# Five entries of a placement table: when the next expert's weight operands are made

## The chip, the cores and the metric

The kernel runs on one core of a Trainium2 chip. The metric is the device time of one execution in microseconds (us): before the change 1099.89 us, the median of three runs (1097.52, 1099.89, 1102.34).

## The reference

Three layers run one after the other on 2304 rows of 512 values. The first two (an attention with exponential features, and a mixture of experts over slots) are not touched. The third is:

```python
logits = x @ w_gate
P = np.exp(logits - logits.max())
for _ in range(8):                       # balancing
    P /= P.sum(1, keepdims=True) + 1e-09
    P /= P.sum(0, keepdims=True) + 1e-09
    P *= N / E
for e in range(E):                       # E = 8 experts, w1[e] 512 x 1024, w2[e] 1024 x 512
    h = np.maximum(x @ w1[e], 0.0)
    out += P[:, e:e + 1] * (h @ w2[e])
```

## The kernel before

**Experts and blocks.** The third layer goes through 8 experts (0 to 7), and through 9 blocks (0 to 8) of 256 rows in each; the code calls a place in it `(blk, k)`, block and product. The hidden block (1024 x 256) is laid out as 2 x 2 quarters, and `h @ w2` is done by a scheme of Strassen's kind: 7 products of sums of quarters in place of 8 products. `PRODUCTS` names for each product k = 0 to 6 the hidden operand, the weight operand and the accumulator:

```python
PRODUCTS = [("a11", "b11", "x"), ("a12", "b21", "z"), ("s2", "t2", "x"), ("s1", "t1", "y"),
            ("s3", "t3", "x"), ("s4", "b22", "y"), ("a22", "t4", "x")]
```

**Operands in two parts.** Each operand is a high part and a low part: ScalarE (ACT) writes the rounded copy, and the low part is the difference. A product is 12 matmuls (high x high, high x low, low x high, over 4 chunks). Four hidden operands (`s1`, `s2`, `s4`, `s3`, in this order) get their low part `hl_s` on GpSimd (POOL); the others, and the sums themselves, are made by VectorE (DVE), which also takes each finished product into the output (`take`: `xo <- x, P, xo`).

**Weight operands.** Those of the next expert are made while this one runs. `w_begin` allocates, `w_sum(e, n)` makes one of four sums t1 to t4 on POOL, in place in the loaded weights (t2 has a tile of its own), and `w_part(e, k)` makes operand k: an ACT copy (`CAST w_b` or `w_t`, 128x1024) and a POOL subtraction on the same tile. The profile's `w_b` are the operands b11, b21 and b22 (k = 0, 1, 5), its `w_t` are t2, t1, t3 and t4 (k = 2, 3, 4, 6). There are 10 operand buffers, and operand k of expert e has number `(7 * e + k) % 10`. So operand k of the next expert, for k = 3 to 6, goes to the buffer of this expert's operand k - 3, and must wait for its last product, which is product k - 3 of block 8.

**What sets the order.** From the middle of the kernel on every engine runs its instructions in the order in which the code writes them (`InOrder`); waits between engines are put in by the framework. The loop at the end of `tile_kernel` writes, for each product: the product and its take; at product 2 the first layer of the next block; one step of the next block's hidden operands (`hidden`); then the sums and operands that the two tables `W_SUMS` and `W_PARTS` name for this place. A key with block 9 is block 0 of the next expert. In block 8 the next expert's first-layer weights are stacked (`make_stack` behind product 0: `ps`, `st`) and spread (`spread_stack` behind product 1: `pr`, and two ACT copies `st <- pr`). While expert 0 runs, DVE also does the balancing of `P` (`sinkhorn`), a few steps at a time. After block 0 of an expert `load_munits` asks for further weights on the SyncE queue; each transfer waits until its buffer is free.

Of the kernel before, what the change touches and what calls it, by code (L numbers as in the profile page):

```python
# [53 lines left out]
def tile_kernel(ctx: ExitStack, tc: tile.TileContext, a):  # L54
# [569 lines left out]
    def w_sum(e, n):  # L624


        w = wsrc[e]
        if n == 0:
            G.tensor_tensor(out=w["t1"], in0=w["t3"], in1=w["b11"], op=ALU.subtract)
        elif n == 1:  # L630
            G.tensor_tensor(out=w["t2"], in0=w["t1"], in1=w["b22"], op=ALU.subtract)
        elif n == 2:
            G.tensor_tensor(out=w["t3"], in0=w["t3"], in1=w["b22"], op=ALU.subtract)
        else:
            G.tensor_tensor(out=w["t4"], in0=w["t4"], in1=w["t2"], op=ALU.add)

    def w_part(e, k):

        name = PRODUCTS[k][1]
        s = wsrc[e][name]  # L640
        n = (7 * e + k) % NW
        w = (cl1 if n < 4 else cl2).tile([128, 2, KH, 256], F32R, tag=f"wo{n}", name=f"w{e}_{name}", bufs=1)
        A.copy(out=w[:, 0], in_=s)
        G.tensor_tensor(out=w[:, 1], in0=s, in1=w[:, 0].bitcast(F32), op=ALU.subtract)
        wop[e, k] = w
        if k == 6:
            wsrc.pop(e)
            for n in range(2):
                unit_t.pop(("moe2_w2", e, n))
# [286 lines left out]
        pass  # L936
    load_munits(4)

    W_SUMS = {(3, 1): 0, (3, 6): 1, (5, 6): 2, (7, 6): 3}
    W_PARTS = {(2, 6): 0, (4, 6): 2, (6, 6): 1, (8, 1): 3, (8, 6): 4, (9, 0): 5, (9, 1): 6}  # L940
    SINK = {0: 1, 1: 2, 6: 2}
    making = iter(())
    for i, (e, blk) in enumerate(blocks):
# [3 lines left out]
        for k in range(7):  # L947
# [10 lines left out]
            next(making, None)  # L958
            if more and (blk, k) in W_SUMS:
                w_sum(e + 1, W_SUMS[blk, k])  # L960
            if more and (blk, k) in W_PARTS:
                w_part(e + 1, W_PARTS[blk, k])
            if e and (blk + 9, k) in W_PARTS:
                w_part(e, W_PARTS[blk + 9, k])
            if e == 0:
# [72 lines left out]
```

## Time and profile before

| | |
|---|---|
| runs (us) | 1102.34, 1097.52, 1099.89 |
| profiled execution | 1099.17 us, span 1097.0 us |
| granted clock of TensorE, mean | 0.994 |
| PE (matmuls) busy | 1053.4 us, 96% |
| DVE, ACT, POOL busy | 67%, 52%, 63% |
| third layer, products | from 281.2 us to the end |
| one `w_sum` or the POOL half of one `w_part` | 2.4 us |
| one `hl_s` pair on POOL | 2.5 to 2.6 us |

The profile shows one execution. Times are us from the start of the span. "PE" is matmuls, "PEld" the loads of their stationary operand, which overlap them. In a timeline a row is the start, the busy time, the engine, the line (all are line 50, a helper that records every operation), the operation, what it writes and reads, and in brackets the idle time of that engine just before it with what ended it. A chain of waits goes back from the end, at each step to what released it. The first-layer matmuls `z<-ct,st` come once per block, between its products 2 and 3, and serve as a mark for its place in time.

### The profile page before, as it was taken

How to read it: one execution, taken by the hardware profiler on the slowest of the kernel's cores; microseconds unless marked ns; L12 is line 12 of the kernel's file. 1: busy time of each engine (PE TensorE's matmuls, PEld its weight loads, DVE VectorE, ACT ScalarE, POOL GpSimd, SP SyncE). 2: the span in 40 equal slices, each digit the busy share in tenths (PEclk: the TensorE clock that was granted, in tenths of full speed). 3: DMA queues.
4: the chain of work that ended last, by engine and by line, in shares of the span. 5: the costliest groups of instructions: out<-in, count | busy, mean ns of one | idle time of the engine just before them, and what ended most of it. 6: DMA issues, size and time to landing. Idle time of an engine off the chain costs nothing.

```text
span 1097.0 us, 23161 instructions
## 1 busy us (share of the span) xinstructions
PE 1053.4 (96%) x9206; PEld 982.4 (90%) x9206; DVE 737.7 (67%) x1526; ACT 569.1 (52%) x1009; POOL 686.8 (63%) x442
## 2 busy tenths in 40 slices
PE   7999999999888899999999999999999999999998
PEld 4788889853888889999999999999999999999998
DVE  6878677750678866766776677567666766676765
ACT  5665544313455556655455455545554564555542
POOL 4776551107555676767767686867677775777443
PEclk9999989999999999999999999999999999999999
DMA  7762215379400040012002200400220022000111
GB/s 261 261 257 85 59 30 208 139 303 370 154 1 1 2 143 12 2 50 105 1 1 78 78 2 1 149 6 2 77 78 1 1 82 73 1 1 21 45 53 59
DMA packets 22571, 89.26 MB, mean 81 GB/s; under 512 B 2752, under 2 KB 5568, under 8 KB 14272
## 3 DMA queue, kind: packets, MB, share of 16 engines
q1 hardware_dynamic: 22176, 87.26, 22.0%
q8 instruction: 73, 1.20, 0.5%
q0 software_dynamic: 288, 0.52, 0.2%
q14 instruction: 34, 0.28, 0.1%
HBM read 83.05 MB, written 4.72 MB: 80 GB/s over the span
## 4 chain that ended last, share of the span: by engine, by line
PE 68%; POOL 15%; issue 6%; DVE 6%; ACT 4%; DMA 1%; SPq 0%; POOLq 0%; ACTq 0%; DVEq 0%
PE x L50 25%; PE y L50 12%; PE z L50 11%; POOL hl_s L50 8%; PE num L271 6%; POOL w_t L50 4%; PE kvacc L179 3%; POOL w_b L50 2%; DVE s L50 2%; PE ut L246 1%; PE ps L50 1%; PE kvp L218 1%; DMA moe_w<-in_moe_w 1%; ACT hh_s L50 1%; DVE xo L50 1%
## 5 line engine op out<-in xcount | busy, mean ns | idle before, releaser
L50 POOL TENSOR_TENSOR hl_s<-s,hh_s 128x512 fp32r<-128x512 f32 x288 | 367.4, 1297 | 240.9 <-ACT hh_s L50 226.5
L50 PE MATMUL x<-w_t,hh_s 128*128 128x256 f32 x1152 | 205.0, 278 | 5.2 <-DVE xo L50 3.9
L50 ACT ACTIVATE hh_s<-s 128x512 fp32r<-128x512 f32 x288 | 175.3, 629 | 52.0 <-DVE s L50 49.3
L50 PEld LDWEIGHTS x<-w_t,hh_s 128*128 128x128 f32 x1152 | 173.9, 188 | 7.2 <-issue 3.2
L50 DVE SCALAR_TENSOR_TENSOR xo<-x,P,xo 128x256 f32<-128x256 f32 x252 | 121.0, 480 | 81.0 <-PE x L50 75.4
L50 ACT ACTIVATE hh_a<-z 128x512 fp32r<-128x512 f32 x216 | 122.2, 600 | 90.5 <-DVE s L50 88.6
L50 ACT ACTIVATE r<-z 128x512 f32<-128x512 f32 x144 | 86.2, 599 | 159.9 <-PE z L50 159.6
L50 DVE SCALAR_TENSOR_TENSOR s<-z,r 128x512 f32<-128x512 f32 x144 | 99.0, 688 | 90.6 <-ACT hh_a L50 86.2
L50 PE MATMUL x<-w_t,hl_s 128*128 128x256 f32 x576 | 159.7, 277 | 0.0
L50 DVE SCALAR_TENSOR_TENSOR hl_a<-z,hh_a 128x512 fp32r<-128x512 f32 x216 | 147.2, 681 | 0.0
L50 DVE SCALAR_TENSOR_TENSOR s<-z,s 128x512 f32<-128x512 f32 x144 | 98.4, 684 | 20.6 <-POOL hl_s L50 19.3
L50 PE MATMUL x<-w_t,hh_a 128*128 128x256 f32 x576 | 104.3, 279 | 5.2 <-POOL w_t L50 4.8
L50 PEld LDWEIGHTS x<-w_t,hl_s 128*128 128x128 f32 x576 | 108.2, 188 | 0.0
L50 PE MATMUL y<-w_b,hh_s 128*128 128x256 f32 x576 | 103.9, 279 | 0.0
L50 PE MATMUL z<-w_b,hh_a 128*128 128x256 f32 x576 | 103.6, 280 | 0.0
L50 PE MATMUL x<-w_b,hh_a 128*128 128x256 f32 x576 | 103.4, 280 | 0.0
L50 PE MATMUL y<-w_t,hh_s 128*128 128x256 f32 x576 | 102.9, 278 | 0.0
L50 PEld LDWEIGHTS x<-w_t,hh_a 128*128 128x128 f32 x576 | 87.6, 188 | 6.8 <-POOL w_t L50 6.2
L50 PEld LDWEIGHTS z<-w_b,hh_a 128*128 128x128 f32 x576 | 87.3, 189 | 2.5 <-issue 2.5
L50 PEld LDWEIGHTS y<-w_b,hh_s 128*128 128x128 f32 x576 | 87.5, 188 | 1.3 <-POOL w_b L50 1.3
L50 PEld LDWEIGHTS x<-w_b,hh_a 128*128 128x128 f32 x576 | 88.0, 190 | 0.0
L50 PEld LDWEIGHTS y<-w_t,hh_s 128*128 128x128 f32 x576 | 87.6, 189 | 0.0
(214 smaller groups left out, 2344.7 us busy)
## 6 DMA issues: line engine op xcount, KB each, us to landing
moe_w<-in_moe_w SPq DMA_DIRECT2D x64, 1024.0 KB, 6.9
vt<-in_vb SPq DMA_DIRECT2D x20, 256.0 KB, 3.6
kt<-in_kT SPq DMA_DIRECT2D x18, 256.0 KB, 3.5
qt<-in_qT SPq DMA_DIRECT2D x18, 256.0 KB, 2.7
out<-xo SPq DMA_DIRECT2D x18, 128.0 KB, 1.7
out<-xo SPq DMA_DIRECT2D x9, 256.0 KB, 2.0
rep<-in_rep POOLq DMA_DIRECT2D x2, 256.0 KB, 6.0
bd<-in_bd SPq DMA_DIRECT2D x1, 384.0 KB, 3.7
```

Of the source, the lines that this page charges most:

```text
L50: return lambda *args, **kwargs: self.tc.keep_in_program_order(make(*args, **kwargs))
L179: PE.matmul(acc[64 * j:64 * j + 64, p * 256:(p + 1) * 256], v[:, (2 * p + j) * D:(2 * p + j + 1) * D], phik[:, 2 * p + j].rearrange("p c f ...
L218: PE.matmul(ps[:, c * 192:(c + 1) * 192], kvt[:, p * 256 + c * 128:p * 256 + (c + 1) * 128], bd[:, p], start=True, stop=True)
L246: PE.transpose(ps[:, j * 128:(j + 1) * 128], uq_t[t][hh][:, j * 128:(j + 1) * 128], ident)
L271: PE.matmul(ps[r0:r1, j * XW:(j + 1) * XW], phiq[:, c, j * 128 + r0:j * 128 + r1], kvs_t[b][:, c, 4 * hh + j, :], start=c == 0, stop=c == 1,)
```

## The change

The entries of the two tables are changed, and nothing else:

```diff
-    W_SUMS = {(3, 1): 0, (3, 6): 1, (5, 6): 2, (7, 6): 3}
-    W_PARTS = {(2, 6): 0, (4, 6): 2, (6, 6): 1, (8, 1): 3, (8, 6): 4, (9, 0): 5, (9, 1): 6}
+    W_SUMS = {(3, 1): 0, (3, 6): 1, (5, 6): 2, (7, 1): 3}
+    W_PARTS = {(2, 6): 0, (4, 6): 2, (6, 6): 1, (8, 0): 3, (8, 1): 4, (8, 6): 5, (9, 0): 6}
```

The last sum (t4) goes from product 6 of block 7 to product 1. Operand 3 (t1) goes from product 1 of block 8 to product 0, operand 4 (t3) from product 6 to product 1, operand 5 (b22) from product 0 of the next expert's block 0 to product 6 of block 8, operand 6 (t4) from product 1 of that block 0 to product 0.

On POOL, from the last low part that is made for block 8 of expert 3 to the first that is made for block 1 of expert 4 (`w4_...` are the weight operands of expert 4; `hl_s1_36` is the low part of s1 for the 36th block counted from 0, which is block 0 of expert 4). Before:

```order
L50 TENSOR_TENSOR hl_s3_35_8679<-s3_35_8661,hh_s3_35_8677 128x512
L50 TENSOR_TENSOR moe2_w2_4_1_7655<-moe2_w2_4_1_7655,t4_7805 128x4x256
L50 TENSOR_TENSOR w4_t1_8743<-moe2_w2_4_0_7653,w4_t1_8743 128x1024
L50 TENSOR_TENSOR hl_s1_36_8797<-s1_36_8774,hh_s1_36_8795 128x512
L50 TENSOR_TENSOR hl_s2_36_8816<-s2_36_8790,hh_s2_36_8814 128x512
L50 TENSOR_TENSOR hl_s4_36_8840<-s4_36_8820,hh_s4_36_8838 128x512
L50 TENSOR_TENSOR hl_s3_36_8859<-s3_36_8841,hh_s3_36_8857 128x512
L50 TENSOR_TENSOR w4_t3_8862<-moe2_w2_4_0_7653,w4_t3_8862 128x1024
L50 TENSOR_TENSOR w4_b22_8879<-moe2_w2_4_1_7655,w4_b22_8879 128x1024
L50 TENSOR_TENSOR w4_t4_8896<-moe2_w2_4_1_7655,w4_t4_8896 128x1024
L50 TENSOR_TENSOR hl_s1_37_8950<-s1_37_8927,hh_s1_37_8948 128x512
```

Now, the same place on POOL:

```order
L50 TENSOR_TENSOR hl_s3_35_8680<-s3_35_8662,hh_s3_35_8678 128x512
L50 TENSOR_TENSOR w4_t1_8717<-moe2_w2_4_0_7653,w4_t1_8717 128x1024
L50 TENSOR_TENSOR w4_t3_8746<-moe2_w2_4_0_7653,w4_t3_8746 128x1024
L50 TENSOR_TENSOR hl_s1_36_8800<-s1_36_8777,hh_s1_36_8798 128x512
L50 TENSOR_TENSOR hl_s2_36_8819<-s2_36_8793,hh_s2_36_8817 128x512
L50 TENSOR_TENSOR hl_s4_36_8843<-s4_36_8823,hh_s4_36_8841 128x512
L50 TENSOR_TENSOR hl_s3_36_8862<-s3_36_8844,hh_s3_36_8860 128x512
L50 TENSOR_TENSOR w4_b22_8865<-moe2_w2_4_1_7655,w4_b22_8865 128x1024
L50 TENSOR_TENSOR w4_t4_8882<-moe2_w2_4_1_7655,w4_t4_8882 128x1024
L50 TENSOR_TENSOR hl_s1_37_8950<-s1_37_8927,hh_s1_37_8948 128x512
```

In block 8 two operands (t1, t3) stand where a sum and one operand stood; ahead of `hl_s1_37` there are two operands instead of three. The sum has gone to the place behind operand 1 (`w4_b21`), ahead of the `hl_s` of block 7.

On ACT, in block 8 of expert 3, with the engines that each instruction waits for (`hh_s3_35` is the high part of s3, `st4` the spread first-layer weights of expert 4). Before:

```order
L50 ACTIVATE hh_s4_35_8658<-s4_35_8640 128x512 [waits PE_49]
L50 ACTIVATE hh_s3_35_8677<-s3_35_8661 128x512 [waits DVE_49,PE_49]
L50 CAST st4_8714<-pr4_0_8731 128x512 [waits PE_49]
L50 CAST st4_8714<-pr4_1_8737 128x512 [waits DVE_49,PE_49]
L50 CAST w4_t1_8743<-moe2_w2_4_0_7653 128x1024
```

Now:

```order
L50 ACTIVATE hh_s4_35_8659<-s4_35_8641 128x512 [waits PE_49]
L50 ACTIVATE hh_s3_35_8678<-s3_35_8662 128x512 [waits DVE_49,PE_49]
L50 CAST w4_t1_8717<-moe2_w2_4_0_7653 128x1024 [waits PE_49]
L50 CAST st4_8714<-pr4_0_8734 128x512 [waits PE_49]
L50 CAST st4_8714<-pr4_1_8740 128x512 [waits DVE_49,PE_49]
L50 CAST w4_t3_8746<-moe2_w2_4_0_7653 128x1024
```

The copy of t1 has moved ahead of the two `st` copies and carries a wait on PE, and the copy of t3 has come into its old place.

## Rows read from the trace of the kernel before

**Rows 1.** Timeline of PEld (start, us, what): first-layer loads, once per block
```profile
401.55 1.01 PEld L50 LDWEIGHTS z<-ct,st 128*128 128x128 f32 x8
414.46 1.01 PEld L50 LDWEIGHTS z<-ct,st 128*128 128x128 f32 x8
...
702.82 1.01 PEld L50 LDWEIGHTS z<-ct,st 128*128 128x128 f32 x8
715.26 1.01 PEld L50 LDWEIGHTS z<-ct,st 128*128 128x128 f32 x8
...
736.22 1.01 PEld L50 LDWEIGHTS z<-ct,st 128*128 128x128 f32 x8
746.70 1.01 PEld L50 LDWEIGHTS z<-ct,st 128*128 128x128 f32 x8
...
1001.46 1.01 PEld L50 LDWEIGHTS z<-ct,st 128*128 128x128 f32 x8
1013.92 1.02 PEld L50 LDWEIGHTS z<-ct,st 128*128 128x128 f32 x8
```

**Rows 2.** Timeline of PEld, expert 3 to 4: loads that stood idle before
```profile
706.87 0.19 PEld L50 LDWEIGHTS y<-w_b,hh_s 128*128 128x128 f32 x1 [0.19 <-POOL w_b L50]
709.21 0.19 PEld L50 LDWEIGHTS x<-w_t,hh_a 128*128 128x128 f32 x1 [0.89 <-POOL w_t L50]
713.88 0.30 PEld L50 LDWEIGHTS x<-w_t,hh_s 128*128 128x128 f32 x2 [0.48 <-issue]
```

**Rows 3.** Chain of waits in the same stretch: start, us, what
```profile
702.10 2.35 POOL w_t L50
704.45 2.37 POOL w_b L50
706.82 2.33 POOL w_t L50
709.15 2.51 POOL hl_s L50 x2
```

**Rows 4.** Timeline of DVE, the same stretch
```profile
698.55 0.68 DVE L50 SCALAR_TENSOR_TENSOR s<-z,r 128x512 f32<-128x512 f32 x1
700.41 0.48 DVE L50 SCALAR_TENSOR_TENSOR xo<-x,P,xo 128x256 f32<-128x256 f32 x1 [0.19 <-PE x L50]
710.43 0.69 DVE L50 SCALAR_TENSOR_TENSOR s<-z,s 128x512 f32<-128x512 f32 x1 [2.30 <-POOL hl_s L50]
711.69 0.69 DVE L50 SCALAR_TENSOR_TENSOR s<-z,r 128x512 f32<-128x512 f32 x1 [0.17 <-POOL hl_s L50]
```

**Rows 5.** Timelines of PEld and ACT, block 8 of expert 3
```profile
686.82 1.45 PEld L50 LDWEIGHTS ps<-moe_w,sot 128*32 128x32 f32 x32
...
690.83 1.08 ACT L50 CAST st<-pr 128x512 fp32r<-128x512 f32 x2 [4.55 <-PE pr L50]
```

**Rows 6.** Timeline of POOL, block 3 of expert 4: an earlier sum
```profile
737.92 2.41 POOL L50 TENSOR_TENSOR moe_w<-moe_w 128x1024 f32<-128x1024 f32 x1
```

**Rows 7.** By stretch: us; PE, PEld, DVE, ACT, POOL busy; clock, DMA share, GB/s
```profile
690.00:695.00 5.00, 5.00 (x46) 5.00 (x46) 1.59 (x4) 3.60 (x6) 2.79 (x2) 1.00 0.91 378
```

**Rows 8.** Timelines of POOL, DVE and PEld, blocks 3 and 7 of expert 0
```profile
325.38 2.40 POOL L50 TENSOR_TENSOR moe_w<-moe_w 128x1024 f32<-128x1024 f32 x1
...
325.58 2.36 DVE L50 TENSOR_TENSOR P<-P,cs 128x144 f32<-128x144 f32 x1
...
376.04 0.29 DVE L50 TENSOR_TENSOR P<-P,cs 128x144 f32<-128x144 f32 x1
...
325.42 1.02 PEld L50 LDWEIGHTS z<-ct,st 128*128 128x128 f32 x8
338.58 1.01 PEld L50 LDWEIGHTS z<-ct,st 128*128 128x128 f32 x8
...
363.42 1.01 PEld L50 LDWEIGHTS z<-ct,st 128*128 128x128 f32 x8
375.89 1.03 PEld L50 LDWEIGHTS z<-ct,st 128*128 128x128 f32 x8
```

## The prediction

> **What bounds the kernel now.** I read the table of the page first: the matmul engine PE is busy 96% of the span, so a change can only gain where PE stands still. Then I looked for that place by block. In the last stage each block loads its first-layer weights once (`z<-ct,st`), so the distance between two such loads is the length of a block [rows 1]. An ordinary block lasts 746.70 - 736.22 = 10.48 us. From block 0 to block 1 of a new expert it is 715.26 - 702.82 = 12.44 us, and for the last expert 1013.92 - 1001.46 = 12.46 us. The two are the same work, 84 product matmuls and 8 of the first layer, so 1.97 us (the mean) is standstill. Six experts (2 to 7) show 12.44 to 12.46; expert 1 shows 414.46 - 401.55 = 12.91, 2.43 over. Together 6 x 1.97 + 2.43 = 14.25 us, 1.3% of the span. That is the most that removing this standstill can give.
>
> Third, the loads in that stretch which stood idle before [rows 2]: 0.19 us before product 5 (waiting for POOL's `w_b`), 0.89 before product 6 (POOL's `w_t`), 0.48 before product 2 of block 1, where the profile names no releaser. Smaller gaps make up the rest of 1.97. Fourth, the chain of waits through that stretch [rows 3]: it doesn't run over PE but over POOL, three low halves of operands back to back (2.35, 2.37, 2.33 us), and only then the `hl_s` pair for the next block, from 709.15. Fifth, who waits behind that pair [rows 4]: DVE's s4 starts at 710.43 after 2.30 idle us, released by `hl_s`, and s3 at 711.69. DVE runs in order, so the first take of block 1 comes after them, and PE's product 2 must wait for that take, because products 0 and 2 add into the same sums. So the unnamed third gap has the same origin: POOL's queue at the block boundary is one operand too long.
>
> **The change part by part.** No instruction is added or removed. Per expert, one sum and four operand steps (an ACT copy and a POOL subtraction each) come sooner.
>
> *Operands 5 and 6.* In block 0 POOL now finds two operands instead of three ahead of `hl_s`. What was operand 4's slot from 702.10 becomes operand 5's, what was 5's becomes 6's, and `hl_s` starts where 6 started. By the lengths in [rows 3]: b22 done at 704.45, t4 at 706.82, `hl_s` from 706.82 instead of 709.15. PE asks for b22 at 706.87 - 0.19 = 706.68, so 2.2 us are spare. It asks for t4 at 709.21 - 0.89 - 0.19 = 708.13, so 1.3 us are spare. Both gaps close. What is late next is DVE's s3: 711.69 - 2.35 = 709.34, against 698.55 + 10.48 = 709.03 on time [rows 4]: 0.31 late. The first take of the block has 0.19 of idle time before it (700.41), so it is 0.12 late: 700.41 + 10.48 + 0.12 = 711.01, done at 711.49. PE's product 2 stands 715.26 - 713.88 = 1.38 ahead of its marker, and with the gaps gone the marker is due at 702.82 + 10.48 = 713.30, so product 2 asks at 711.92. 0.43 us are spare, and the third gap closes too. Gain 1.97 for each of six experts: 11.82. In block 0 of expert 1, ACT's scaling of the output rows stands between s3 and the take, so part of the 0.31 can reach PE. I take 0.1 and a gain of 2.3 (bounds 2.43 - 0.31 = 2.12 and 2.43).
>
> *Operand 4* takes the slot at the second product that operand 3 had, on ACT behind the `st` copies and on POOL ahead of `hl_s`. Same engine, same lengths: nothing, both ways.
>
> *Operand 3, after the first product of block 8.* On POOL it takes the time at which the last sum ran. On ACT its copy now stands ahead of the `st` copies, and it has a wait that is new there: its buffer is the one that product 0 has just read. Behind it on ACT are the `st` copies, which the first layer of the next expert needs. ACT stands idle for 4.55 us before these copies (690.83), and PE is past product 0 at 686.82, when `ps` starts [rows 5]. A copy of this many elements takes about 1.08 (the two `st` halves, same row), so it ends near 688.0 with 2.8 us spare. I take nothing. If the release came only with `pr`, as for the copies, all 1.08 would show, seven times: 7.6 us as the upper bound. It can't gain: no load in [rows 2] waited for operand 3.
>
> *The last sum, five products sooner,* stands on POOL between operand 1 and the `hl_s` pairs of block 7. Block 3 has had that very sequence all along, and in expert 4 the sum at 737.92 [rows 6] lies in an ordinary block of 10.48 us [rows 1]. So it costs nothing in experts 1 to 6 (bounds 0, and the price of expert 0 six times, 4.2). In expert 0 it does: there DVE also runs the balancing steps, and `P<-P,cs` beside the sum of block 3 took 2.36 us, from 325.58 until POOL was done, where alone it took 0.29 (376.04) [rows 8]. That stretch was 338.58 - 325.42 = 13.16 us long, against 12.47 (363.42 to 375.89) without a sum. The moved sum, behind operand 1, would start at about 375.8 and cover the step at 376.04. I charge 0.7 once.
>
> On this the Trainium skill (GPSIMD Engine Reference, Key points) says that GpSimd shares its SBUF interfaces with VectorE, and contends with instructions that read two SBUF inputs or run in a 2-port mode. The trace agrees: `P<-P,cs`, both inputs in SBUF, waited POOL out. By that rule the later experts pay nothing, since their DVE operations read one input from PSUM.
>
> *Weight transfers.* The tiles of the parts are free sooner, so two transfers of an expert's weights start sooner, one of them right beside block 8. With the transfer engines 91% busy PE was still busy 5.00 of 5.00 us [rows 7]; I take nothing.
>
> **Sum.** 11.8 + 2.3 - 0.7 = 13.4 us. The profiled execution took 1099.17 (span 1097.0 and 2.17 around it), which gives 1085.8. The median of the three runs lies 0.7 higher, which would give 1086.5; I say 1086.
>
> **Rivals.**
> - *The gap moves to DVE.* `hl_s` starts sooner, but the takes stay late, and the third gap, 0.48 with the small ones around it about 0.55, stays in seven experts: 3.9 us, so 1090. For it: s3 is 0.31 late by my own count. Against: 0.43 spare.
> - *The moved sum holds DVE up in every expert,* not in expert 0 alone: 4.2 us more, 1090. For it: 2.36 against 0.29. Against: the block of 10.48 with a sum in it.
> - *Slower: operand 3's copy blocks ACT.* If its wait is let go only when PE has finished product 2 (about 692.6), `st` would follow at 693.7 and the first layer at 694.8 instead of 692.34: 2.46 x 7 = 17.2 lost, 13.4 gained, 1103. It costs something from a release after 690.83 - 1.08 = 689.75 on, and eats the whole gain from about 691.7 on. For it: the copy at that place had no wait on PE, and now it has. Against: the wait is for product 0 alone, and PE is past it by 686.82.
> - *It doesn't do what it says:* the wait for POOL is only the last of several at that place, and another input, also late, holds PE: 1097 to 1100. Against: [rows 3] is one unbroken chain on POOL, with no other engine in it.
>
> **How the numbers follow.** Forecast 0.80; gap moves to DVE 0.08; sum in every expert 0.05; no effect 0.04; slower 0.03. The forecast's own range is 1084 to 1088.5: the runs before spread by 2.4 either way, and the 0.7 may not show or show twice. Taking in part of the two rivals at 1090, the range is 1083.5 to 1091. About 0.5% (5.5 us) is what a measurement can tell from no change. The first three cases lie beyond it: 0.93 faster. No effect and most of the slower rival lie within it: 0.05. Slower by more: 0.02.
>
> **What would show it.** Right: from block 0 to block 1 about 10.5 us in experts 2 to 7; in block 0 no load waits for POOL's `w_b` or `w_t`; POOL has two operands ahead of `hl_s`, and DVE's s4 waits next to nothing; in block 8 ACT has `w_t` ahead of `st`, and `st` still follows `pr` at once; in block 7 of expert 0 a `P<-P,cs` of some 2.4 us and about 0.7 us more to block 8. Wrong: a load before product 2 that still stands idle for half a microsecond; `st` copies released by `w_t`; blocks 7 to 8 longer in later experts; a stretch from block 0 to 1 above 11 us.

## The result, and the profile after the change

The changed kernel takes 1086.64 us (median of four runs, 1084.58 to 1088.38) against 1099.54 before (also four runs, 1097.52 to 1102.34): a ratio of 0.9871, 95% interval 0.9851 to 0.9892. Forecast were 1086 us and a range of 1083.5 to 1091. The profiled execution has a span of 1084.3 us, 12.7 less. All times in this document are of executions with a mean granted clock of 0.988 or more; one execution of the last version below, at 0.721, took 1855.61 us and is left out.

The first-layer loads once per block (timeline of PEld, start and duration in us), at the places of [rows 1]:

```profile
402.82 1.01 PEld L50 LDWEIGHTS z<-ct,st 128*128 128x128 f32 x8
413.42 1.02 PEld L50 LDWEIGHTS z<-ct,st 128*128 128x128 f32 x8
...
698.04 1.01 PEld L50 LDWEIGHTS z<-ct,st 128*128 128x128 f32 x8
708.52 1.01 PEld L50 LDWEIGHTS z<-ct,st 128*128 128x128 f32 x8
...
729.48 1.01 PEld L50 LDWEIGHTS z<-ct,st 128*128 128x128 f32 x8
739.96 1.01 PEld L50 LDWEIGHTS z<-ct,st 128*128 128x128 f32 x8
...
990.78 1.01 PEld L50 LDWEIGHTS z<-ct,st 128*128 128x128 f32 x8
1001.26 1.01 PEld L50 LDWEIGHTS z<-ct,st 128*128 128x128 f32 x8
```

From block 0 to block 1 of expert 4 it is 708.52 - 698.04 = 10.48 us, an ordinary block, and the same in all of experts 2 to 7. In expert 1 it is 10.60. Block 3 of expert 4 (729.48 to 739.96), which has had a sum at its start all along, is unchanged. Now the same stretch on POOL, the counterpart of [rows 3]:

```profile
697.26 2.41 POOL L50 TENSOR_TENSOR w_b<-moe_w,w_b 128x1024 fp32r<-128x1024 f32 x1
699.62 2.43 POOL L50 TENSOR_TENSOR w_t<-moe_w,w_t 128x1024 fp32r<-128x1024 f32 x1
701.99 2.57 POOL L50 TENSOR_TENSOR hl_s<-s,hh_s 128x512 fp32r<-128x512 f32 x2
```

Two operands stand ahead of the `hl_s` pair, with no idle time between them. The chain of waits of [rows 3] went over POOL here; now, in order of time (start, duration, what), it stays on PE:

```profile
696.96 1.36 PE x L50 x12
698.32 0.94 PE z L50 x8
...
```

And DVE, the counterpart of [rows 4]:

```profile
693.77 0.69 DVE L50 SCALAR_TENSOR_TENSOR s<-z,r 128x512 f32<-128x512 f32 x1
695.63 0.48 DVE L50 SCALAR_TENSOR_TENSOR xo<-x,P,xo 128x256 f32<-128x256 f32 x1 [0.19 <-PE x L50]
...
703.34 0.69 DVE L50 SCALAR_TENSOR_TENSOR s<-z,s 128x512 f32<-128x512 f32 x1
704.59 0.69 DVE L50 SCALAR_TENSOR_TENSOR s<-z,r 128x512 f32<-128x512 f32 x1 [0.17 <-POOL hl_s L50]
...
706.19 0.47 DVE L50 SCALAR_TENSOR_TENSOR xo<-x,P,xo 128x256 f32<-128x256 f32 x1
```

s4 (703.34) no longer waits 2.30 us; s3 (704.59) is 704.59 - (693.77 + 10.48) = 0.34 us late, the first take of block 1 (706.19) 0.08 us. In the table of waits by releaser none of PE's waits in the third layer is for POOL any more.

Why DVE has to wait for POOL at all stands in the code: `raw` in `hidden` has three buffers (`bufs=3`), so s4 takes the buffer of s1 and s3 that of s2, and each can be written only when POOL's `hl_s` has read the earlier sum. A fourth buffer, another way to set DVE free, was not tried.

**Block by block.** The lengths between marks, in us:

| stretch | before | after | forecast |
|---|---|---|---|
| block 0 to 1, experts 2 to 7, sum of six | 74.70 | 62.88 | -11.82 |
| block 0 to 1, expert 1 | 12.91 | 10.60 | -2.3 |
| block 7 to 8, expert 0 | 15.18 | 15.59 | +0.7 |
| all other blocks | 685.81 | 686.11 | 0 |
| first mark to last | 788.60 | 775.18 | -13.4 |

So -13.42 measured between first and last mark, against -13.4. That the two agree to 0.02 is in part chance: the stretch in expert 0 cost 0.29 less than was charged, and the other blocks took 0.30 more. Of this 0.16 lie in one block of expert 2 (10.60 before, 10.76 after), which also differs between the two profiles of one kernel in the first experiment (10.56 and 10.76). The span shows 0.7 less of it because the first mark lies at 288.96 instead of 288.22, behind two layers that the change doesn't touch.

### The profile page after: what moved, and what is told of

Read it like the earlier page. It is cut to its first block, busy times and chain, and to the rows that moved or that the text cites. A ratio compares the mean times of both kernels' runs of the same rounds, so it can differ in the third digit from the quotient of the medians.

```text
span 1084.3 us, 23161 instructions
## 1 busy us (share of the span) xinstructions
PE 1050.2 (97%) x9206; PEld 982.8 (91%) x9206; DVE 742.1 (68%) x1526; ACT 571.4 (53%) x1009; POOL 688.3 (63%) x442
## 4 chain that ended last, share of the span: by engine, by line
PE 80%; POOL 6%; issue 5%; DVE 4%; ACT 2%; DMA 2%; SPq 0%; POOLq 0%; ACTq 0%; DVEq 0%
PE x L50 31%; PE y L50 15%; PE z L50 13%; PE num L271 6%; POOL hl_s L50 3%; PE kvacc L179 2%; PE ut L246 1%; PE ps L50 1%; PE kvp L218 1%; DMA moe_w<-in_moe_w 1%; PE ph L50 1%; PE pk L142 1%; PE pk L144 1%; POOL zs L197 1%; DVE s L50 1%
```

## The experiments

The forecast held, but its reading of the cause had parts that a right sum doesn't prove: that POOL's queue ahead of `hl_s` is all of it, and not ACT's copies, the sum's move or the lateness of the operands themselves. Times are against the kernel before on the same chip; block lengths come from the profile of each run.

**Operands moved, the sum not.**

```diff
-    W_SUMS = {(3, 1): 0, (3, 6): 1, (5, 6): 2, (7, 1): 3}
+    W_SUMS = {(3, 1): 0, (3, 6): 1, (5, 6): 2, (7, 6): 3}
```

> The four operands at the new places, the last sum back at product 6 of block 7. Theory (POOL has one operand fewer ahead of hl_s in block 0, and that is the whole gain): block 0 to 1 stays at 10.48 us in experts 2 to 7, and the stretch from block 7 to 8 of expert 0 falls back from 15.59 to about 15.2, so a span 0.4 us below the changed kernel's. On POOL sum, t1 and t3 then stand ahead of block 0's hl_s: they would end about 0.1 us before hl_s is due. Rival (the sum had to go sooner to make room for operand 4): hl_s of block 0 and all behind it come later, several tenths in each of seven experts, 2 to 5 us in all.

Measured: 1085.48 us, ratio 0.9869 (0.9853 to 0.9886), span 1083.7. Block 0 to 1 is 10.48 in experts 2 to 7 and 10.60 in expert 1; block 7 to 8 of expert 0 is back at 15.18. POOL in block 8 of expert 3 and block 0 of expert 4:

```profile
682.99 2.40 POOL L50 TENSOR_TENSOR moe_w<-moe_w,t 128x1024 f32<-128x1024 f32 x1
685.34 4.77 POOL L50 TENSOR_TENSOR w_t<-moe_w,w_t 128x1024 fp32r<-128x1024 f32 x2
690.46 2.56 POOL L50 TENSOR_TENSOR hl_s<-s,hh_s 128x512 fp32r<-128x512 f32 x2 [0.35 <-ACT hh_s L50]
```

Sum, t1 and t3 stand back to back and end 0.35 us before the `hl_s` pair (about 0.1 was expected), which is released by ACT as ever. The sum's move carried nothing and cost expert 0 the 0.41 us. A second time, beside the last version below:

> The four operands at the new places with the last sum at its old one, beside the version above on the same chip: block 7 to 8 of expert 0 at 15.2 us, block 0 to 1 at 10.48, expert 1's three blocks at 11.15, span near 1083.7.

It took 1085.87 us, ratio 0.9867 (0.9842 to 0.9892), span 1083.8, with the same block lengths (15.18, 10.48, and 11.14 to 11.18).

**The sum moved, the operands not.**

```diff
-    W_PARTS = {(2, 6): 0, (4, 6): 2, (6, 6): 1, (8, 0): 3, (8, 1): 4, (8, 6): 5, (9, 0): 6}
+    W_PARTS = {(2, 6): 0, (4, 6): 2, (6, 6): 1, (8, 1): 3, (8, 6): 4, (9, 0): 5, (9, 1): 6}
```

> Only the last sum at its new place, the operands as before. Theory: block 0 to 1 stays at 12.44 us, POOL's chain of three operands unchanged, and expert 0 pays 0.4 to 0.7 us between block 7 and 8: 1099.5 to 1100.5. Rival (the sum's move frees POOL and carries part of the gain): block 0 to 1 shorter than 12.4.

Measured: 1101.84 us, ratio 1.0014 (1.0001 to 1.0027). Block 0 to 1 stays at 12.43 to 12.46, block 7 to 8 of expert 0 is 15.59. By the blocks that is the theory's point; the time lies 1.3 us above the 1099.5 to 1100.5 that it gave. (The span of 1102.3 is longer than these blocks explain, since the marks add up to before's plus 0.4; the rest lies ahead of the first block, where nothing was changed.)

**ACT's copies moved, POOL's part not.** `w_part` is split, and the four subtractions, and the last sum, are written at the places that they had before:

```diff
...
+    W_LOWS = {(8, 1): 3, (8, 6): 4, (9, 0): 5, (9, 1): 6}
-                w_part(e + 1, W_PARTS[blk, k])
+                w_part(e + 1, W_PARTS[blk, k], blk < 8)
+            if more and (blk, k) in W_LOWS:
+                w_low(e + 1, W_LOWS[blk, k])
...
```

> ACT's four copies at the new places, POOL's sum and its four subtractions at the old ones. Theory (POOL's queue): no gain, block 0 to 1 stays at 12.44 us, time within 0.3% of before. Rival (ACT: with one copy fewer in block 0 it is sooner at the hidden operands): block 0 to 1 at 10.5, time as the changed kernel's, near 1086.6.

Measured: 1099.42 us, ratio 0.9998 (0.9983 to 1.0012). Block 0 to 1 is 12.43 to 12.44. The loads that stood idle (timeline of PEld, expert 3 to 4) are those of [rows 2], with the same waits for POOL:

```profile
707.95 0.19 PEld L50 LDWEIGHTS y<-w_b,hh_s 128*128 128x128 f32 x1 [0.18 <-POOL w_b L50]
710.29 0.19 PEld L50 LDWEIGHTS x<-w_t,hh_a 128*128 128x128 f32 x1 [0.86 <-POOL w_t L50]
714.96 0.30 PEld L50 LDWEIGHTS x<-w_t,hh_s 128*128 128x128 f32 x2 [0.61 <-issue]
```

Copies done sooner on ACT are worth nothing while POOL's order stays. The rival on ACT has fallen.

**Operand 6 back at product 1 of block 0.**

```diff
-... (8, 6): 5, (9, 0): 6}
+... (8, 6): 5, (9, 1): 6}
```

> As the changed kernel, but operand 6 (t4) asked for at product 1 of block 0 again, as before the change. Theory: POOL's order is the same and it is busy with operand 5 until then, so nothing moves: block 0 to 1 at 10.48, span 1084.3 within 1. Rival (each product that an operand is asked for sooner counts): up to one product, 1.36 us, more in each of seven experts, 9 us.

Measured in one execution: 1085.45 us, span 1083.2 (1.1 below the changed kernel's; the first mark lies 1.2 us sooner), block 0 to 1 at 10.47 to 10.48 in experts 2 to 7. Of the five entries that were moved, this one's move changed nothing: POOL's order is the same with and without it.

**A filler ahead of `hl_s`.** The sharpest question was whether PE lost its 1.97 us to operands that were late or to the `hl_s` behind them. So the changed kernel gets one, two or four needless subtractions on POOL, behind operand 6:

```diff
                 w_part(e, W_PARTS[blk + 9, k])
+                for _ in range(2):           # 1, 2 or 4
+                    G.tensor_tensor(out=fill, in0=fill, in1=fill, op=ALU.subtract)
```

One:

> As the changed kernel, with one needless POOL subtraction of 128x224 (about 0.6 us by the lengths of 128x512 and 128x1024) behind operand 6 and ahead of block 0's hl_s. It holds up no weight operand, only hl_s. Theory (the stall comes through hl_s, DVE's s4 and s3 and the first take; the take has 0.4 us to spare in experts 2 to 7, none in expert 1): block 0 to 1 longer by 0.6 - 0.4 = 0.2 us in experts 2 to 7, by 0.6 in expert 1. Rival (PE waited for b22 and t4 themselves, the rest was a consequence): no change, 10.48.

Two:

> Two such fillers, 1.25 us. Theory: block 0 to 1 longer by 0.85 us in experts 2 to 7, so 11.3, and by 1.25 in expert 1. Rival: no change, 10.48.

Four:

> Four such fillers, 2.5 us, as much POOL time as the operand that the change took away from this place. Theory: block 0 to 1 longer by 2.1 us in experts 2 to 7, so 12.6, as long as before the change though no operand is late. Rival: no change, 10.48; between them, the share of the 1.97 us that the late operands had of themselves.

The second column is the start of `hl_s` less that of the first filler (of t4 in the last row), the last one the mean over 10.48.

| fillers | `hl_s` put off by | block 0 to 1, expert 2 to 7 | over 10.48 |
|---|---|---|---|
| 0 (changed kernel) | 0 | 10.48 | 0 |
| 1 | 0.52 | 10.60 to 10.67 | 0.17 |
| 2 | 1.17 | 11.24 to 11.29 | 0.79 |
| 4 | 2.45 | 12.54 to 12.57 (expert 5, left out of the mean: 12.97) | 2.08 |
| kernel before: t4 in that place | 2.33 | 12.44 to 12.46 | 1.97 |

Single executions: spans 1089.6, 1092.9 and 1102.3 (in the first two the first mark comes 3.7 and 2.9 us later than in the changed kernel). In every row the block grows by the delay of `hl_s` less 0.35 to 0.38 us. In expert 1, where nothing to spare was expected, it grows from 10.60 to 11.07 and 11.70 with one and two fillers, 0.47 and 1.10 us for 0.52 and 1.15. (What expert 5, and expert 1 with four fillers, 13.78, have beyond that is the matter of the last section.) With two, on POOL, DVE and PEld of experts 3 to 4, the first and the last row being the marks:

```profile
703.53 1.01 PEld L50 LDWEIGHTS z<-ct,st 128*128 128x128 f32 x8
...
707.47 1.22 POOL L50 TENSOR_TENSOR fill<-fill 128x224 f32<-128x224 f32 x2
708.65 2.55 POOL L50 TENSOR_TENSOR hl_s<-s,hh_s 128x512 fp32r<-128x512 f32 x2
...
709.97 0.69 DVE L50 SCALAR_TENSOR_TENSOR s<-z,s 128x512 f32<-128x512 f32 x1 [1.14 <-POOL hl_s L50]
...
713.42 0.30 PEld L50 LDWEIGHTS x<-w_t,hh_s 128*128 128x128 f32 x2 [0.70 <-issue]
714.80 1.01 PEld L50 LDWEIGHTS z<-ct,st 128*128 128x128 f32 x8
```

The fillers end, `hl_s` starts, s4 waits 1.14 us for it, and the only idle load between the marks is that of product 2 in block 1, 0.70 us, again without a releaser's name. No operand is late there. So the direct waits of [rows 2] on `w_b` and `w_t` were not a cost of their own: POOL's queue of 2.33 us too much would have cost the same if these operands had been on time. PE stood a while at each of three places of one delay that was fixed by `hl_s`. The reverse, late operands with `hl_s` on time, was not run; what they would cost alone stays open.

**A version from these findings.** The sum back at its place; and one thing that the block lengths show beside the change: in expert 1 three blocks take 11.15 us, because a copy of operand 0, 2 or 1 stands on ACT ahead of the scaling of the output rows, for which the first take of the next block waits. In experts 1 to 6 these operands are now written one product later:

```diff
-    W_SUMS = {(3, 1): 0, (3, 6): 1, (5, 6): 2, (7, 1): 3}
-    W_PARTS = {(2, 6): 0, (4, 6): 2, (6, 6): 1, (8, 0): 3, (8, 1): 4, (8, 6): 5, (9, 0): 6}
+    W_SUMS = {(3, 1): 0, (3, 6): 1, (5, 6): 2, (7, 6): 3}
+    W_PARTS = {(8, 0): 3, (8, 1): 4, (8, 6): 5, (9, 0): 6}
+    W_FIRST = [{(2, 6): 0, (4, 6): 2, (6, 6): 1}, {(3, 0): 0, (5, 0): 2, (7, 0): 1}]
...
+            if more and (blk, k) in W_FIRST[e > 0]:
+                w_part(e + 1, W_FIRST[e > 0][blk, k])
```

> A version made from the findings: the last sum back at product 6 of block 7, and in experts 1 to 6 operands 0, 2 and 1 asked for after product 0 of blocks 3, 5 and 7, so that on ACT expert 1's scaling of the output rows goes ahead of the copy of the operand. Theory (the three blocks of 11.15 us in expert 1 are one copy, about 0.95 us, ahead of the scaling that the first take waits for): they fall to 10.48, 2.0 us in all, other blocks unchanged, since POOL is still at hl_s when the copy is done; a span of about 1081.9 (before 1097.0, changed kernel 1084.3). Rival (POOL is held up by the later copy): the same blocks or the ones after them stay at 11 us.

Measured: 1084.55 us (median of three, 1082.57 to 1086.16), ratio 0.9852 (0.9825 to 0.988). Its profile is that of the execution left out, so the blocks are read from a second run:

> The version with the operands behind expert 1's scaling once more, for its profile. Theory: three blocks of expert 1 at 10.48 instead of 11.15, span about 1081.9. Rival: they, or the blocks after them, stay at 11.

Measured: 1085.63 us, ratio 0.988 (0.9853 to 0.9908), span 1082.1. The three blocks take 10.48, 10.48 and 10.48, and one beside them 10.82 in place of 10.49: 1.7 us less instead of 2.0. ACT in expert 1, at the end of block 2, in the changed kernel:

```profile
431.45 1.04 ACT L50 CAST w_b<-moe_w 128x1024 fp32r<-128x1024 f32 x1
432.40 1.33 ACT L50 ACTIVATE xo<-xo,P 128x512 f32<-128x512 f32 x2
```

and in this version, with POOL and PEld behind it:

```profile
431.15 1.33 ACT L50 ACTIVATE xo<-xo,P 128x512 f32<-128x512 f32 x2
432.37 1.04 ACT L50 CAST w_b<-moe_w 128x1024 fp32r<-128x1024 f32 x1
...
433.49 2.40 POOL L50 TENSOR_TENSOR w_b<-moe_w,w_b 128x1024 fp32r<-128x1024 f32 x1
434.09 1.01 PEld L50 LDWEIGHTS z<-ct,st 128*128 128x128 f32 x8
435.97 2.42 POOL L50 TENSOR_TENSOR moe_w<-moe_w 128x1024 f32<-128x1024 f32 x1
438.35 2.55 POOL L50 TENSOR_TENSOR hl_s<-s,hh_s 128x512 fp32r<-128x512 f32 x2
...
443.54 0.30 PEld L50 LDWEIGHTS x<-w_t,hh_s 128*128 128x128 f32 x2 [0.26 <-DVE xo L50]
444.91 1.01 PEld L50 LDWEIGHTS z<-ct,st 128*128 128x128 f32 x8
```

The scaling stands ahead of the copy. The 10.82 (434.09 to 444.91) is the rival's point, in one block of the three: there the operand and the first sum stand on POOL ahead of `hl_s`. That starts 4.26 us after the mark, where in the changed kernel it is 3.48 (435.09 to 438.57), and PE waits for DVE's take once more: the path of the main finding.

Between first and last mark it is 2.4 us less than in the changed kernel (772.78 against 775.18; span 2.2 less): 1.7, 0.41 in expert 0, and 0.3 in small differences. The times don't show it: the ratios 0.9852 and 0.988 lie on either side of the changed kernel's 0.9871. It is shown by the blocks alone.

## Why the prediction was right

*Block 0 to 1, the term of 11.82.* Right to the hundredth. The steps as forecast and as measured: t4 done 1.3 us before PE asks for it (701.99 on POOL, product 6 at about 703.4: 1.4); s3 0.31 late (0.34); take 0.12 late (0.08); spare time before product 2 0.43 (0.35 to 0.38, from the fillers). The prediction named POOL's queue as the origin of all three gaps, and then counted them, each with its spare time, as closing one by one. The fillers show that one delay is enough: that of the `hl_s` pair, less 0.35 to 0.38 us, is what the block loses, whichever load shows the idle time.

*Expert 1.* 2.31 for 2.3. The 0.1 that the scaling on ACT was to let through is 0.12 (10.60 against 10.48).

*Operand 3's copy and its new wait*, the rival on the slower side. ACT in block 8 of expert 3, the counterpart of [rows 5]:

```profile
682.15 1.05 ACT L50 CAST w_t<-moe_w 128x1024 fp32r<-128x1024 f32 x1 [0.26 <-PE x L50]
686.05 1.08 ACT L50 CAST st<-pr 128x512 fp32r<-128x512 f32 x2 [2.85 <-PE pr L50]
```

The copy waited 0.26 us for PE's product 0 and was done 2.85 us before `pr` released the `st` copies: 2.8 was forecast. Block 8 kept its 13.74 us in experts 1 to 6.

*The moved sum.* In experts 1 to 6 nothing, as the block that already had one [rows 6] said; blocks 7 to 8 are unchanged. In expert 0 the mechanism was right and the size was not: the term of 0.7 measured 0.41. After the change, with the mark of block 7, the step of DVE that came to lie beside the sum, and PE's load of product 6:

```profile
376.75 1.03 PEld L50 LDWEIGHTS z<-ct,st 128*128 128x128 f32 x8
376.91 2.36 DVE L50 TENSOR_TENSOR P<-P,cs 128x144 f32<-128x144 f32 x1
382.44 0.30 PEld L50 LDWEIGHTS x<-w_t,hh_a 128*128 128x128 f32 x2 [0.43 <-DVE xo L50]
```

and that load in the kernel before, in block 3 with a sum, and in blocks 6 and 7 without one:

```profile
331.11 0.30 PEld L50 LDWEIGHTS x<-w_t,hh_a 128*128 128x128 f32 x2 [0.56 <-DVE xo L50]
...
368.47 0.30 PEld L50 LDWEIGHTS x<-w_t,hh_a 128*128 128x128 f32 x2
...
381.09 0.31 PEld L50 LDWEIGHTS x<-w_t,hh_a 128*128 128x128 f32 x2
```

`P<-P,cs` took 2.36 us instead of the 0.29 of [rows 8], as in block 3, and through DVE's takes it held PE at product 6 until 5.69 us after the mark, in block 3 (331.11 - 325.42) and in block 7 (382.44 - 376.75) alike. But without a sum PE comes to product 6 later in block 7, 5.20 us after the mark (381.09 - 375.89), than in block 6, 5.05 (368.47 - 363.42). So the same lateness takes less from it: 0.49 us instead of 0.64, of which 0.41 are left at the next mark, where block 3 keeps its 0.69. The price had been read off block 3, which is quicker up to that place; why block 7 is slower stays open. That the sum does it is shown by the runs with the sum alone (15.59) and with the operands alone (15.18), and by all others here: 15.51 to 15.69 in the six profiles with the moved sum, 15.17 to 15.18 in the five without.

*Weight transfers.* Nothing, as said: blocks 8 and 0 of experts 2 to 7 have their lengths to the hundredth.

*The rival that the gap moves to DVE* was right about the place and wrong about the margin: of s3's 0.34 us of lateness 0.08 reached the take, and 0.35 to 0.38 us more could still be taken up before product 2. With one filler, which puts `hl_s` off by 0.52 us, it begins to come true.

## What to carry to other kernels

Compare equal stretches (here block against block) before you add up waits: the rows that name a releaser made up 1.08 of the 1.97 us, and the part without a name had the same cause. In a queue that runs in order ask what stands behind the late work: the operands on POOL mattered less for themselves than for the `hl_s` that they kept waiting. And count the slack that a fix leaves (under 0.4 us here), because the next operation put into that place will pay for all beyond it.

## What the runs showed of the hardware that was not expected

With four fillers the stall before product 2 reached 1.96 to 1.97 us in experts 2 to 7 and 2.42 us in expert 1, and behind it in experts 1, 5 and 7 the next block was long too (11.25, 11.63 and 12.03 us). In expert 7, and then in expert 4 (busy time by stretch: us; PE, PEld, DVE, ACT, POOL busy; granted clock; DMA share, GB/s; and the timeline of PEld):

```profile
1017.00:1030.00 13.00, 13.00 (x103) 13.00 (x102) 7.39 (x14) 5.15 (x9) 5.45 (x5) 0.87 0.12 42
...
1016.26 0.30 PEld L50 LDWEIGHTS x<-w_t,hh_s 128*128 128x128 f32 x2 [1.96 <-ACT hh_s L50]
1017.67 1.83 PEld L50 LDWEIGHTS z<-ct,st 128*128 128x128 f32 x8
1029.70 1.01 PEld L50 LDWEIGHTS z<-ct,st 128*128 128x128 f32 x8
...
717.00:730.00 13.00, 13.00 (x116) 13.00 (x115) 8.16 (x16) 6.62 (x12) 5.10 (x4) 1.00 0.00 1
...
715.68 0.30 PEld L50 LDWEIGHTS x<-w_t,hh_s 128*128 128x128 f32 x2 [1.97 <-ACT hh_s L50]
717.09 1.02 PEld L50 LDWEIGHTS z<-ct,st 128*128 128x128 f32 x8
727.58 1.01 PEld L50 LDWEIGHTS z<-ct,st 128*128 128x128 f32 x8
```

In expert 7 the granted clock over these 13 us is 0.87, and the eight loads of the first layer take 1.83 us where they take 1.01 at full clock: for a part of the stretch TensorE ran at the lower of its two levels, 1.2 GHz instead of 2.4, after it had stood still for 1.96 us. In experts 1 and 5 the same loads take 1.78 and 1.82 us. In each of the three it cost about 1.55 us more than the stall (12.03 - 10.48 in expert 7). Experts 2, 3, 4 and 6 had a stall of 1.97 us and kept a clock of 1.00, as the kernel before did with 0.90 us as its longest gap at this place. So after a stall of this length the clock may fall or not; which of the two it is, these runs don't tell.
